# Two weight conversions leave the attention stage, and the joint unit's masks and operands are loaded later

## The chip, the cores and the metric

One core of a Trainium2 chip runs the program. The metric is device time in microseconds of that core. The engines are called PE (TensorE, matmuls), DVE (VectorE), ACT (ScalarE), POOL (GpSimd) and SP (SyncE, which here only issues DMAs).

## What is computed

Causal block attention in blocks of 64 positions (4 batches, 8 heads, 576 positions, 64 per head), then two feed-forward stages on the 2304 x 512 result:

```
scores = scale * q @ k^T, masked where block_i < block_j; attn = softmax(scores)
x  = (attn @ v), heads side by side                          # 4 x 576 x 512
k  = max((mu_k*x + (1-mu_k)*x_prev) @ w_k, 0)                # 512 -> 1024
r  = sigmoid((mu_r*x + (1-mu_r)*x_prev) @ w_r)
x  = r * (k*k @ w_v)                                         # 1024 -> 512
out = x + max(layernorm(x)*g @ w_ch1, 0) @ w_ch2             # 512 -> 2048 -> 512
```

Inputs and output are float32. Most matmuls are done as three passes over a high part and a low part of each operand (high x high, high x low, low x high), so every weight and every activation has to be split into two tiles before PE can use it.

## The kernel before, in words

**Attention** runs as 34 units in a hand-written order (the loop over i from line 973 on). A unit is one head of one batch, except unit 0 and unit 15, which are "z" units: they hold the first 64 positions of all heads of a batch. Unit 15 is the **joint unit**, with batches 1, 2 and 3 in one. In turn i the kernel emits the score product of unit i+1 (em_A), the low-part correction of unit i with its exponential (em_B, ACT tile e), the row maxima of unit i+1 (chain: DVE tiles part, r, m, then the product on DVE line 451 that writes the maxima into QK or, for the joint unit, into wv), the product with V (em_PV), and the split of the operands of the units i+2 and i+3 on POOL (line 44, tiles QK and kq). The heads' operands arrive by DMAs on POOL's queue (line 257, tile kq, two heads at a time) and on SP's queue (tiles raw and V).

The joint unit borrows the tiles of the weight w_v, which are free until after attention: KZ lies in wv[0] and its low parts LZ and QZ in wv[1]. Its **masks** (masks_z, line 236; the DMA is line 237) are one POOL DMA into the lower 64 partitions of LZ and QZ. Each of its three **operands** a = 1, 2, 3 (joint_z, line 294) takes a POOL DMA (line 301), two SP DMAs (lines 302 and 303), an ACT copy and two subtractions, one on POOL and one on DVE or POOL. MASKS_Z and READY_Z (lines 910 and 911) name the turns at which these are emitted: load, ACT copy, the first subtraction, the second subtraction, and the engines of the two.

**Weight conversion.** A weight matrix is cut into pieces of 128 x 512. load_split (line 86) makes of one piece the steps load (an SP DMA of 512 KB into a byte buffer raw), above and below (two reads of the exponent byte), expo, bits (DVE line 135), high and low. During attention above, below and high run on ACT, expo and low on POOL, and bits on DVE. Behind attention above runs on DVE (line 117), below on ACT into PSUM, expo and bits on DVE (lines 129 and 135), high and low on POOL (lines 139 and 44). PIECES (line 904) says at which turns of attention the steps of the first eight pieces are emitted: one letter a turn, l load, 1 and 2 above and below, x expo, b bits, h high, w low (V is low on DVE). The pieces come in the order w_r (four), w_k columns 0 to 511 (four, rows k = 0 to 3), w_k columns 512 to 1023 (four), w_v (eight).

The pieces that PIECES does not name are converted behind attention by a small pipeline (Convert, line 152): each conv.step() advances every piece under way by one step, oldest first, and starts the next. A piece started at step n has its low part emitted at step n+4. These steps stand between the products: six of w_r (em_r), four of w_k for the first group of tokens (em_h, two column blocks m0 to m0+1 each, with out_h behind it: three ACT passes and the DVE subtraction of line 44, tile k), and the first product with w_v (em_v0), which calls step(m) ahead of each of its eight row blocks m. xq.step() in the same places advances prep, which forms the next group's inputs (tiles mix and y). Then the second feed-forward stage runs to the end.

```
def step(self, start=True, keep=0):
    for j in self.going:
        if len(j) > keep:
            f = j.pop(0)
```

Of the kernel before, what the change touches and what calls it, by code (L numbers as in the profile page):

```python
# [32 lines left out]
def attention_moe_kernel(ctx, tc, raw_d, dup_d, raw0_d, dup0_d, v_d, v0_d, msk_d, mz_d, vec_d, eye_d, wk_d, wv_d, wr_d, wc1_d, wc2_d, out_d):  # L33
    nc = tc.nc
# [169 lines left out]
    V = [cp.tile([128, 5, 256], F32, name=f"V{i}") for i in range(2)]  # L204
# [25 lines left out]
    T = {}  # L230

    def masks(i):
        nc.gpsimd.dma_start(out=QK[i][64:128], in_=msk_d)
        nc.gpsimd.memset(KL[i].bitcast(F32)[0:64, 576:640], 0.0)
# [324 lines left out]
    def preps(g, c, X):  # L559
        return [lambda kk=kk: prep(g, kk, c, X) for kk in range(4)]  # L560
# [323 lines left out]
    def em_c2(c, G, ts):  # L884
# [17 lines left out]


    PIECES = [
        (1, "l.12xbhw"), (4, "l12xbhw"), (7, "l..12xbh.w"), (17, "l12xbhw"),
        (20, "l.12xbhw"), (23, "l12xb.hw"), (25, "L.12xb.hw"), (29, "l12xbhV"),
    ]


    MASKS_Z = 2  # L910
    READY_Z = (5, 8.5, 9.5, 9.25, nc.gpsimd, nc.vector), (8, 12, 11.5, 11.25, nc.gpsimd, nc.vector), (10, 13, 14, 13, nc.gpsimd, nc.gpsimd)
    TAIL_Z = 18, 18, 18.5, 20, 23, 22.5, 21, 23.9, 22.9, 21.9
    with tc.manual_schedule():

        plan = {}
        T["attention"] = True
        for i, p in PIECES:
            load, (above, below), (expo, bits), high, low = jobs.pop(0)
            steps = {"l": load, "1": above, "2": below, "x": expo, "b": bits, "h": high, "w": low, "L": load, "V": lambda low=low: low(nc.vector)}
            for x, c in enumerate(p):  # L920
                if c != ".":
                    plan.setdefault(i + x + {"b": .25, "L": .5, "V": .5}.get(c, 0), []).append(steps[c])
        conv = Convert(jobs)
        load_raw(units[0])
        load_raw(units[1])
# [43 lines left out]
        masks(0)  # L969
        plan.setdefault(MASKS_Z, []).append(lambda: masks_z(1, 2))  # L970
        for a in (1, 2, 3):
            joint_z(a, READY_Z[a - 1])
        for i in range(N + 2):
# [23 lines left out]
            if i == N - 2:  # L997
# [8 lines left out]
                xq = Convert(rest)  # L1006
# [52 lines left out]
            if late:  # L1059
                take_z(units[i - 2], 2)  # L1060
                L = tail_z(units[i - 2])
                for a in sorted(set(TAIL_Z)):
                    plan[a] = [f for x, f in zip(TAIL_Z, L) if x == a] + plan.get(a, [])
            if 1 <= i < N - 1 and not mid:
                em_PV(units[i - 1])
                if i == 1:
                    take_z(units[0], 0)
                    L = tail_z(units[0])
# [39 lines left out]
        xq = Convert(preps(2, MR, XC) + preps(3, MR, XD) + preps(4, MR, XA) + preps(5, MR, XC) + preps(HORD[0], MK, XB))  # L1108
        for g, X in enumerate((XA, XB, XC, XD, XA, XC)):
            s = em_r(X)  # L1110
            if g > 1:
                out_r(g - 1, s0)
            xq.some(2)
            if g == 0:
                out_r(g, s)
            if g == 5:

                es_xa.close()
                rh = opened(es_xa, "rh", 3)
                a, b = lambda: rh.tile([128, 4096], I8, name="rawh"), lambda: stg2.tile([128, 4096], I8, name="raw8")  # L1120
                T["raws"] = [a, a, a, b, b, a]
                conv.ahead()
            if g:
                conv.step()
            xq.some(2)
            if g in (2, 4, 5):
                conv.step()
            s0 = s
        xq.all()
# [2 lines left out]
        for j, g in enumerate(HORD):  # L1132
            for m0 in (0, 2, 4, 6):
                s = em_h(X2[j % 2], m0)
                if j == 0 and m0 == 0:
                    out_r(NG - 1, s0)
                out_h(m0, s)
                if j == 0:
                    conv.step()
                    if m0 == 0:  # L1140
                        conv.step()
                if j + 1 == NG and m0 == 0:
                    ln_scale(0, 3 * g)
                    ln_scale(3 * g + 3, NTILE)
            if j + 1 == NG:
                break
            xq = Convert(preps(HORD[j + 1], MK, X2[(j + 1) % 2]))
            if j == 0:

                def step(m):  # L1150
                    if m < 3:
                        conv.step()
                    if m == 1:
                        es_xa.close()
                        xa = opened(es_x, "xa2")
                        X2[1].extend(xa.tile([128, 4, GT], F32R, name=f"y{j}") for j in range(2))
                    xq.step()

                p = em_v0(step)
                assert not conv.jobs and not conv.going and not T["raws"]  # L1160
                T["beside"] = False
                xq.all()
                for t in range(3):
                    out_v(g, t, p[t])
                load_r(HORD[3], rp)
                continue
            em_v(g, 0)
            xq.all()
            if j + 2 == NG:
                conv = Convert(chunk_jobs(0))  # L1170
                conv.some(2, keep=2)
            em_v(g, 1)
            if j + 2 == NG:
                conv.some(2, start=False, keep=2)
            em_v(g, 2)
            if j < 2:
                load_r(HORD[j + 3], rp)
            elif j + 2 == NG:
                load_r(HORD[j + 1], rp)
# [7 lines left out]
        g = HORD[-1]  # L1187
# [257 lines left out]
```

## Time and profile before

| | |
|---|---|
| median of 3 runs | 833.28 us (833.15 to 833.73) |
| the profiled execution's own time | 833.41 us |
| its span, first to last instruction | 831.3 us |
| PE busy | 797.0 us (96%), 3774 matmuls |
| DVE, ACT, POOL busy | 562.9, 410.7, 342.0 us |
| granted TensorE clock | 1.00 over the whole span |

The span falls into attention (to about 181 us), the products with w_r (to 231), w_k for the first group (to 249), the first product with w_v (to 265) and the rest, in which PE is nearly without a gap. In the timelines a row is an engine's instruction or a merged run of like ones; the bracket behind it tells how long the engine stood idle before it and what ended that. In the chain of waits each row is the piece of work on which the end hung in that stretch.

### The profile page before, as it was taken

What the parts mean: (1) busy time and instruction counts of PE and PEld (TensorE: products, weight loads), DVE (VectorE), ACT (ScalarE), POOL (GpSimd) and SP (SyncE); (2) the same over time, 40 slices, a digit from 0 to 9 for tenths busy, and PEclk for the clock granted to TensorE, in tenths of its full rate; (3) what the DMA queues carried; (4) which work ended last, traced back from release to release, by engine and by line L of the source; (5) the groups of instructions that cost most, each with busy time, mean ns of one, the idle gap of its engine ahead of it and who ended that gap; (6) DMA issues with size and microseconds to landing.
All of it is one profiled execution on the core that took longest, in us unless ns stands there. A gap on an engine that the chain in (4) does not pass through costs nothing.

```text
span 831.3 us, 10607 instructions
## 1 busy us (share of the span) xinstructions
PE 797.0 (96%) x3774; PEld 660.9 (80%) x3774; DVE 562.9 (68%) x1011; ACT 410.7 (49%) x700; POOL 342.0 (41%) x303
## 2 busy tenths in 40 slices
PE   3988899999999999999999999999999999999998
PEld 3666666668898998998988887888888888878886
DVE  6889799987788334244386768768575677757545
ACT  6887788878774534525544423233241334343211
POOL 5797889956585011011021659432080630010100
PEclk9999999999999999999999999999999999999999
DMA  8998788821340110012424111604024166160443
GB/s 216 308 335 272 220 259 253 271 83 76 113 178 28 62 64 25 13 39 69 160 95 170 51 52 52 252 24 162 18 102 151 51 205 250 52 236 18 149 155 127
DMA packets 47636, 112.60 MB, mean 135 GB/s; under 512 B 5408, under 2 KB 19872, under 8 KB 45280
## 3 DMA queue, kind: packets, MB, share of 16 engines
q1 hardware_dynamic: 37792, 64.40, 23.8%
q0 software_dynamic: 9360, 45.17, 16.0%
q10 hardware_dynamic: 432, 2.36, 0.7%
q8 instruction: 30, 0.49, 0.2%
q14 instruction: 22, 0.18, 0.1%
HBM read 91.62 MB, written 20.30 MB: 135 GB/s over the span
## 4 chain that ended last, share of the span: by engine, by line
PE 71%; DVE 14%; ACT 8%; issue 4%; DMA 1%; POOL 1%; ACTq 0%; SPq 0%; DVEq 0%; POOLq 0%
PE ph L363 22%; PE po L363 21%; PE s L363 16%; PE p L363 11%; DVE part L418 5%; ACT r L41 2%; ACT e L41 2%; DVE mix L553 1%; DVE QK L451 1%; DVE a L135 1%; DMA raw<-in_raw_dram 1%; PE ph L714 1%; ACT p L41 1%; DVE m L449 1%; DVE acc L896 1%
## 5 line engine op out<-in xcount | busy, mean ns | idle before, releaser
L363 PE MATMUL po<-c,h 128*128 128x512 f32 x864 | 207.9, 392 | 1.7 <-DVE acc L896 1.1
L363 PEld LDWEIGHTS po<-c,h 128*128 128x128 f32 x864 | 161.0, 188 | 39.6 <-DVE acc L896 5.3
L363 PE MATMUL ph<-x,c 128*128 128x512 f32 (+1 forms) x552 | 116.6, 353 | 0.0
L896 DVE TENSOR_TENSOR acc<-po,acc 128x512 f32<-128x512 f32 x144 | 94.7, 685 | 23.0 <-PE po L363 21.9
L363 PEld LDWEIGHTS ph<-x,c 128*128 128x128 f32 x552 | 91.4, 188 | 15.3
L363 PE MATMUL p<-e,V 128*128 128x512 f32 (+1 forms) x310 | 89.4, 435 | 0.0
L363 PE MATMUL p<-wv,k 128*128 128x512 f32 x360 | 82.9, 390 | 0.0
L363 PEld LDWEIGHTS p<-e,V 128*128 128x128 f32 x310 | 54.6, 190 | 30.8 <-issue 25.9
L363 PEld LDWEIGHTS p<-wv,k 128*128 128x128 f32 x360 | 67.4, 188 | 13.8
L44 DVE TENSOR_TENSOR k<-a,k 128x768 fp32r<-128x768 f32 x24 | 23.8, 991 | 73.4 <-ACT a L41 73.4
L41 ACT ACTIVATE h<-ph 128x512 fp32r<-128x512 f32 (+1 forms) x53 | 28.2, 532 | 89.1 <-PE ph L363 89.1
L41 ACT ACTIVATE a<-raw,ce 128x512 f32<-128x512 int8 (+1 forms) x80 | 57.7, 753 | 18.5 <-DVE a L135 10.9
L418 DVE TRANSPOSE_TENSOR_REDUCE part<-s 128x14 f32<-128x448 f32 (+4 forms) x160 | 65.1, 468 | 1.6 <-PE s L363 0.7
L41 ACT ACTIVATE u<-ph 128x512 f32<-128x512 f32 x27 | 16.1, 596 | 87.6 <-PE ph L363 86.3
L41 ACT ACTIVATE e<-s 128x1536 f32<-128x1536 f32 (+1 forms) x34 | 48.4, 1423 | 11.3 <-PE s L363 6.1
L363 PE MATMUL s<-x,wk 128*128 128x384 f32 x288 | 51.7, 338 | 0.9 <-POOL x L44 0.7
L363 PEld LDWEIGHTS s<-x,wk 128*128 128x128 f32 x288 | 50.7, 188 | 1.8 <-POOL x L44 1.0
L363 PE MATMUL s<-y,wk 128*128 128x384 f32 x288 | 51.2, 338 | 0.0
L363 PEld LDWEIGHTS s<-y,wk 128*128 128x128 f32 x288 | 50.8, 188 | 0.2
L814 POOL DMA_DIRECT2D s<-s_scr x12 | 6.4, 535 | 108.0 <-PE ph L363 108.0
L41 ACT ACTIVATE a<-s 128x768 f32<-128x768 f32 x24 | 19.5, 813 | 63.2 <-PE s L363 60.8
L44 POOL TENSOR_TENSOR x<-mix,x 128x384 fp32r<-128x384 f32 x18 | 18.9, 1058 | 75.1 <-ACT x L41 71.3
(178 smaller groups left out, 1410.8 us busy)
## 6 DMA issues: line engine op xcount, KB each, us to landing
kq<-in_dup_dram POOLq DMA_DIRECT2D x15, 1088.0 KB, 7.0
s<-s_scr POOLq DMA_DIRECT2D x13, 1024.0 KB, 7.0
raw<-in_raw_dram SPq DMA_DIRECT2D x32, 288.0 KB, 5.3
raw<-in_w_ch_dram SPq DMA_DIRECT2D x16, 511.6 KB, 3.5
raw<-in_w_ch_dram SPq DMA_DIRECT2D x32, 255.6 KB, 3.9
V<-in_v_dram SPq DMA_DIRECT2D x16, 320.0 KB, 6.4
s_scr<-s POOLq DMA_DIRECT2D x5, 1024.0 KB, 6.3
x_scr<-r SPq DMA_DIRECT2D x18, 256.0 KB, 2.0
```

Of the source, the lines that this page charges most:

```text
L41: nc.scalar.activation(out=out, in_=in_, func=func, **kw)
L44: eng.tensor_tensor(out=out, in0=in0, in1=in1.bitcast(F32), op=ALU.subtract)
L135: stt(out=st["a2"].bitcast(I32), in0=w3, scalar=5, in1=st["a1"].bitcast(I32), op0=ALU.logical_shift_right, op1=ALU.bitwise_or)
L363: nc.tensor.matmul(out=out, lhsT=lhsT, rhs=rhs, start=start, stop=stop, **kw)
L418: red(out=pt[0:kp, b0:b0 + w // 32, j], in_=v3(s[0:kp, o:o + w]), axis=AX.X, op=ALU.max, apply_transpose=True)
L449: lambda: red(out=m, in_=r4[0:32, :, 0:ng], axis=AX.X, op=ALU.max),
L451: lambda x=x: tt(out=v3(dst)[:, x:x + 16], in0=m[:, x:x + 16].unsqueeze(2).to_broadcast([32, 16, 32]), in1=s[64:96, 512:544].unsqueeze(1). ...
L553: stt(out=m[:, o:o + w], in0=XT[b][:, kk, q0:q0 + w], scalar=omm[:, c + kk:c + kk + 1], in1=y[:, o:o + w], op0=ALU.mult, op1=ALU.add)
L714: nc.tensor.transpose(out=pt[kk][:, 128 * x:128 * x + 128], in_=z[:, 128 * kk:128 * kk + 128], identity=eye)
L814: nc.gpsimd.dma_start(out=SF[i].bitcast(F32), in_=s_scr[PAIRS.index(pr), i])
L896: tt(out=acc[i], in0=p, in1=acc[i], op=ALU.add)
```

## The change

MASKS_Z goes from 2 to 12. Of the joint unit's operands, a = 1 has its three loads one turn later and its ACT copy at 10 instead of 8.5; a = 2 has its loads and both subtractions one turn later; a = 3 stays. PIECES loses its entries at 7 and at 29, so the pieces behind the second move up one place each (the entry at 17 now takes the third piece of w_r, and so on) and the pieces k = 2 and 3 of w_k's first columns are left to the pipeline behind attention, which has 14 pieces instead of 12. Of the pipeline's steps eight stood beside the products with w_r, five behind the blocks of w_k and three in the first product with w_v; now it is seven, five and six, and in that last product prep starts one row block later.

```diff
     PIECES = [
-        (1, "l.12xbhw"), (4, "l12xbhw"), (7, "l..12xbh.w"), (17, "l12xbhw"),
-        (20, "l.12xbhw"), (23, "l12xb.hw"), (25, "L.12xb.hw"), (29, "l12xbhV"),
+        (1, "l.12xbhw"), (4, "l12xbhw"), (17, "l12xbhw"),
+        (20, "l.12xbhw"), (23, "l12xb.hw"), (25, "L.12xb.hw"),
     ]
-    MASKS_Z = 2
-    READY_Z = (5, 8.5, 9.5, 9.25, nc.gpsimd, nc.vector), (8, 12, 11.5, 11.25, nc.gpsimd, nc.vector), (10, 13, 14, 13, nc.gpsimd, nc.gpsimd)
+    MASKS_Z = 12
+    READY_Z = (6, 10, 9.5, 9.25, nc.gpsimd, nc.vector), (9, 12, 12.5, 12.25, nc.gpsimd, nc.vector), (10, 13, 14, 13, nc.gpsimd, nc.gpsimd)
...
-                T["raws"] = [a, a, a, b, b, a]
+                T["raws"] = [a, a, a, b, b, a, a, b]
                 conv.ahead()
             if g:
                 conv.step()
             xq.some(2)
-            if g in (2, 4, 5):
+            if g in (2, 4):
                 conv.step()
...
                 def step(m):
-                    if m < 3:
+                    if m < 6:
                         conv.step()
-                    if m == 1:
+                    if m == 3:
                         es_xa.close()
...
-                    xq.step()
+                    if m:
+                        xq.step()
```

PE's order does not change. Two places of the other engines' order follow; a number behind a tile's name tells tiles of one name apart.

POOL, turns 10 to 13 of attention, before (kq and QK are the heads' splits, XT<-XT,RB scales a finished head, wv_84 and wv_83 are the joint unit's tiles, a_698 is a piece's expo):

```order
L44 TENSOR_TENSOR kq<-raw,kq 64x512
L511 TENSOR_TENSOR XT_92<-XT_92,RB_128 128x512
L511 TENSOR_TENSOR XT_92<-XT_92,RB_129 128x512
L44 TENSOR_TENSOR wv_84<-XT_95,wv_83 64x512
L44 TENSOR_TENSOR QK_137<-raw,kq 64x576
L44 TENSOR_TENSOR kq<-raw,kq 64x512
L257 DMA kq<-in_dup_dram 128x2x1088
L131 TENSOR_TENSOR a_698<-a_698,a_743 128x512
L44 TENSOR_TENSOR QK_138<-raw,kq 64x576
L44 TENSOR_TENSOR wv_83<-XT_95,wv_83 64x512
```

The same place in the change:

```order
L44 TENSOR_TENSOR kq<-raw,kq 64x512
L511 TENSOR_TENSOR XT_92<-XT_92,RB_128 128x512
L511 TENSOR_TENSOR XT_92<-XT_92,RB_129 128x512
L44 TENSOR_TENSOR QK_137<-raw,kq 64x576
L44 TENSOR_TENSOR kq<-raw,kq 64x512
L257 DMA kq<-in_dup_dram 128x2x1088
L237 DMA wv_84<-in_mz_dram 64x2x1024
L44 TENSOR_TENSOR wv_84<-XT_95,wv_83 64x512
L44 TENSOR_TENSOR QK_138<-raw,kq 64x576
L44 TENSOR_TENSOR wv_83<-XT_95,wv_83 64x512
```

The subtraction of operand 2 is behind the pair's DMA instead of three instructions ahead of it, the masks' DMA stands right behind that of the pair, and the expo of the piece that started at 7 is gone.

DVE, from the subtraction of the last out_h of the first group on, before (L129 is expo, L135 bits, L117 the next piece's above; mix belongs to prep):

```order
L44 TENSOR_TENSOR k_1868<-a,k_1867 128x768
L129 SCALAR_TENSOR_TENSOR a_2445<-a_2445,p 128x512
L135 SCALAR_TENSOR_TENSOR a_2447<-raw_2368,a_2445 128x512
L117 TENSOR_SCALAR a_2484<-rawh 128x512
L129 SCALAR_TENSOR_TENSOR a_2484<-a_2484,p 128x512
L135 SCALAR_TENSOR_TENSOR a_2486<-rawh,a_2484 128x512
L553 SCALAR_TENSOR_TENSOR mix<-XT_94,omm,mix 128x192
```

The same place in the change, from the third of the pieces that follow that subtraction on (the two ahead of it have the same three rows each):

```order
L129 SCALAR_TENSOR_TENSOR a_2467<-a_2467,p 128x512
L135 SCALAR_TENSOR_TENSOR a_2469<-rawh,a_2467 128x512
L117 TENSOR_SCALAR a_2487<-rawh 128x512
L129 SCALAR_TENSOR_TENSOR a_2487<-a_2487,p 128x512
L135 SCALAR_TENSOR_TENSOR a_2489<-rawh,a_2487 128x512
L117 TENSOR_SCALAR a_2508<-raw_2472 128x512
L553 SCALAR_TENSOR_TENSOR mix<-XT_94,omm,mix 128x192
L553 SCALAR_TENSOR_TENSOR mix<-XT_95,omm,mix 128x192
L129 SCALAR_TENSOR_TENSOR a_2508<-a_2508,p 128x512
L135 SCALAR_TENSOR_TENSOR a_2510<-raw_2472,a_2508 128x512
L553 SCALAR_TENSOR_TENSOR mix<-XT_94,omm,mix 128x192
```

Two pieces stood behind that subtraction before, and five do now, with two of prep's additions between the fourth and the fifth.

## Rows read from the trace of the kernel before

**Rows 1.** Busy us of PE, PEld, DVE, ACT, POOL (count), clock, DMA share, GB/s.
```profile
12.00:84.00 72.00, 62.09 (x284) 45.75 (x285) 62.17 (x156) 57.16 (x106) 58.00 (x53) 1.00 0.96 292
...
231.00:249.00 18.00, 17.10 (x96) 16.46 (x95) 14.73 (x16) 12.12 (x16) 15.75 (x14) 1.00 0.48 179
249.00:265.00 16.00, 16.00 (x72) 13.23 (x71) 13.49 (x19) 8.74 (x18) 11.71 (x11) 1.00 0.01 1
```

**Rows 2.** Chain of waits, turns 11 to 15: start us, us, engine, tile, line.
```profile
71.13 1.58 DVE wv L44
...
76.97 0.96 PE s L363 x5
77.94 2.72 PE p L363 x10
80.66 2.16 PE s L363 x18
...
82.90 1.45 ACT e L41
...
85.43 1.89 DVE wv L451 x3
```

**Rows 3.** ACT timeline, turn 5: start, us, what, [idle before <-releaser].
```profile
40.95 0.76 ACT L41 ACTIVATE a<-raw,ce 128x512 int32<-128x512 int8 x1 [0.89 <-DMA raw<-in_w_r_dram]
```

**Rows 4.** POOL timeline, turn 2.
```profile
22.98 0.64 POOL L237 DMA_DIRECT2D wv<-in_mz_dram  x1
...
29.39 1.27 POOL L44 TENSOR_TENSOR kq<-raw,kq 64x512 fp32r<-64x512 f32 x1 [4.31 <-DMA kq<-in_dup_dram]
```

**Rows 5.** POOL timeline, turn 8.
```profile
53.07 0.58 POOL L301 DMA_DIRECT2D wv<-in_dup_dram  x1
```

**Rows 6.** DVE timeline, turns 8 and 13.
```profile
55.61 1.39 DVE L135 SCALAR_TENSOR_TENSOR a<-raw,a 128x512 int32<-128x512 int32 x1
...
81.21 0.69 DVE L135 SCALAR_TENSOR_TENSOR a<-raw,a 128x512 int32<-128x512 int32 x1
```

**Rows 7.** POOL timeline, turns 11 to 13.
```profile
69.69 1.08 POOL L44 TENSOR_TENSOR wv<-XT,wv 64x512 fp32r<-64x512 f32 x1
...
73.78 0.76 POOL L257 DMA_DIRECT2D kq<-in_dup_dram  x1
...
83.11 1.27 POOL L44 TENSOR_TENSOR kq<-raw,kq 64x512 fp32r<-64x512 f32 x1 [4.71 <-DMA kq<-in_dup_dram]
```

**Rows 8.** DMA issues, 12 to 100 us: count, KB each, median us to landing.
```profile
wv<-in_mz_dram POOLq DMA_DIRECT2D x1, 512.0 KB, 9.1
```

**Rows 9.** PE timeline, the first wv product.
```profile
248.93 16.52 PE L363 MATMUL s<-wv,k 128*128 128x512 f32 x72
```

**Rows 10.** DVE timeline, the wk product and the first wv product.
```profile
238.66 1.34 DVE L44 TENSOR_TENSOR k<-a,k 128x768 fp32r<-128x768 f32 x1 [1.92 <-ACT a L41]
...
254.37 1.02 DVE L135 SCALAR_TENSOR_TENSOR a<-raw,a 128x512 int32<-128x512 int32 x1
255.42 0.43 DVE L117 TENSOR_SCALAR a<-rawh 128x512 f32<-128x512 int8 x1
255.95 0.69 DVE L129 SCALAR_TENSOR_TENSOR a<-a,p 128x512 int32<-128x512 f32 x1
256.74 1.52 DVE L135 SCALAR_TENSOR_TENSOR a<-rawh,a 128x512 int32<-128x512 int32 x1
258.18 2.82 DVE L553 SCALAR_TENSOR_TENSOR mix<-XT,omm,mix 128x192 f32<-128x192 f32 x4
```

**Rows 11.** Tile wv, 228 to 266 us: duration ns min/median/max, first and last start.
```profile
L139 POOL TENSOR_SCALAR wv<-a x8: 626/851/854, 236.4 to 258.3; 128x512 fp32r<-128x512 f32 x8
L44 POOL TENSOR_TENSOR wv<-a,wv x8: 1300/1598/2094, 237.3 to 259.2; 128x512 fp32r<-128x512 f32 x8
```

**Rows 12.** POOL timeline, the first wv product.
```profile
256.41 1.31 POOL L44 TENSOR_TENSOR wv<-a,wv 128x512 fp32r<-128x512 f32 x1
...
259.15 1.30 POOL L44 TENSOR_TENSOR wv<-a,wv 128x512 fp32r<-128x512 f32 x1
```

More of the change, by code (lines that the diff above doesn't have):

```diff
@@ L918, in attention_moe_kernel @@
             load, (above, below), (expo, bits), high, low = jobs.pop(0)
-            steps = {"l": load, "1": above, "2": below, "x": expo, "b": bits, "h": high, "w": low, "L": load, "V": lambda low=low: low(nc.vector)}
+            steps = {"l": load, "1": above, "2": below, "x": expo, "b": bits, "h": high, "w": low, "L": load}
             for x, c in enumerate(p):
                 if c != ".":
-                    plan.setdefault(i + x + {"b": .25, "L": .5, "V": .5}.get(c, 0), []).append(steps[c])
+                    plan.setdefault(i + x + {"b": .25, "L": .5}.get(c, 0), []).append(steps[c])
         conv = Convert(jobs)
```

## The prediction

> **What bounds the kernel now.** I read the busy times by stage first, to see where PE has gaps at all. In attention it has: from 12 to 84 us PE is busy 62.09 of 72 us, DVE 62.17 and POOL 58.00, with the DMA engines at 0.96 [rows 1]. Under the first w_k product it has 17.10 of 18 us, and under the first w_v product 16.00 of 16 [rows 1]. So an earlier finish in attention is a gain, and behind attention only a new wait can change the time.
>
> Next the chain of waits, to see what fills attention. It runs over DVE and ACT in a ring: row maxima, copies, maxima again, the product with the maxima, then the next unit. A DVE instruction put between two units lengthens the ring whole: operand 2's subtraction stands in the chain with 1.58 us [rows 2]. Where the joint unit's scores come in, the chain runs over PE instead: 0.96, 2.72 and 2.16 us from the correction of unit 13 to that of unit 14, then ACT's exponential at 82.90, and at 85.43 DVE writes the joint unit's maxima into wv [rows 2].
>
> Last the timelines of DVE and POOL under the first w_v product. What the reader is to see there is that the two hold each other up: bits takes 0.69 us with POOL idle [rows 6], and 1.52 beside POOL, where it ends 0.54 us after POOL's low part [rows 10, 12].
>
> **What the change does in attention.**
>
> *Early loads.* The masks' DMA leaves turn 2. There POOL stood 4.31 us for a pair of heads that competed with it [rows 4], and three turns later ACT stood 0.89 us for a weight piece, just ahead of an exponential on the chain [rows 3]. With 512 KB [rows 8] less to move, the whole queue runs ahead. The 0.89 is the most it can give, 0 the least, if the piece is late for its own reasons; I take 0.4. POOL's issue of the masks, 0.64 us [rows 4], was hidden in its idle time.
>
> *Turn 8.* Operand 2's DMA issue (0.58 us of POOL [rows 5]) leaves the place ahead of the split that held bits up: 1.39 us there against 0.69 with POOL idle [rows 6]. The gain is 0 to 0.7; I take 0.4. ACT's moved copy and the SP loads of the first and second operands have turns to spare: nothing.
>
> *Turns 11 to 13.* Operand 2's DVE subtraction leaves turn 11, which frees 1.58 us, and returns in turn 12. There the ring of unit 14 gets it, while PE's own chain of 0.96, 2.72 and 2.16 us [rows 2] has become the longer one. If it costs nothing beyond PE's chain, the exponential of unit 14 comes 1.6 earlier. If it takes 1.58 again, unit 14's maxima start where they do now; the piece's bits (0.69 at 81.21 [rows 6]) lies behind them and isn't waited for, and PE's correction then ends 0.6 us earlier, since it no longer queues behind 2.72 and 2.16. I take 1.0. POOL loses operand 2's subtraction of 1.08 in turn 11 and an expo, gains the masks' issue and that subtraction in turn 12, and then stands 4.71 us for a pair anyway [rows 7]: no cost.
>
> *The piece at 29.* Its bits and its low part lie behind the last correction, from which on PE has no gap until the w_k product; its ACT steps at turns 30 and 31 stand ahead of exponentials that wait for PE. Nothing. The same goes for the high and low parts of the piece at 7, in turns 14 and 16. Together attention gives 1.8 us, with bounds of 0.6 and 3.2.
>
> **What it does behind attention.** w_k's two extra pieces come first and are in time: their low parts are emitted beside the products with w_r. But every later piece is late by them. Behind the last out_h subtraction of the first group stood two pieces, and now five, as the order shows. POOL ended the last low part of w_v at 259.15 + 1.30 = 260.45 [rows 12]. PE takes 16.52 / 8 = 2.07 us for each row block of w_v [rows 9], so it needs that last part at 248.93 + 7 x 2.07 + 0.2 = 263.6: a margin of 3.2 us. In the change the piece that ends at that place is k = 4, and three follow.
>
> Each costs a period of DVE and POOL together: from the end of bits at 254.37 + 1.02 to that at 256.74 + 1.52, 2.87 us [rows 10]. POOL makes high, then low, and the next bits ends only 0.54 us after low. The last period also holds two of prep's additions; four of them took 2.82 us [rows 10], so two are 1.4, of which I take 0.9, as part lies beside POOL's copies. On the other side POOL is idle when out_h's first subtraction comes, because its next high part has to wait for a bits behind it: the 1.34 us subtraction and the 1.02 us bits beside it [rows 10] each lose an estimated 0.3 (bits' 1.02 against 0.69 [rows 6]). So the last low part lands at 260.45 - 0.6 + 2 x 2.87 + 3.77 = 269.4 in this trace's time, and PE waits 269.4 - 263.6 = **5.8 us** in all, spread over the row blocks k = 2 to 7.
>
> Bounds: the least is a piece at DVE's own pace, 0.43 + 0.69 + 0.69 [rows 6, 10] and some 0.3 between, 2.1 us. Three of these with the additions free leave 260.45 - 0.6 + 6.3 - 263.6 = 2.6. The most is 2.87 a piece with 1.4 and without the 0.6: 6.9. I stay at 5.8, since two periods in a row show 2.87 in the very place that is now repeated. Prep's late inputs for the next group are covered by the same wait, and the second stage has room.
>
> By the Trainium skill (SBUF — State Buffer, "Who interferes with whom") the later of two such instructions on VectorE and GpSimd blocks until the earlier has finished. By that rule the four instructions of a piece would stand in a row, and the sum would come out 0.9 us higher, as worked out at the second rival. The trace doesn't bear out the full block: beside POOL bits ends 0.54 us after the low part, sooner than the 0.69 it needs alone [rows 6, 10, 12].
>
> **Sum.** 833.41 - 1.8 + 5.8 = 837.4 for the profiled execution, which lies 0.13 above the median; so **837.3 us**. The bounds are 833.41 - 3.2 + 2.6 = 832.8 and 833.41 - 0.6 + 6.9 = 839.7.
>
> **The rivals.**
>
> *The masks land late.* They are now issued behind a pair's DMA at 73.78 + 0.76 [rows 7], or 1.1 us sooner for the missing subtraction. Their DMA took 9.1 us from issue to landing [rows 8], so they land at 82.6 to 83.6. DVE needs them at 85.43 [rows 2] less the gain of 1.8, at 83.6. The pair ahead of them was waited for until 83.11 [rows 7]. If they land 1.8 us late, ahead of everything else on DVE, attention gives nothing: 839.1 us. It decides from a landing after 83.6. The Trainium skill (DMA: Bandwidth & Descriptors, "Issuing engines are not separate DMA queues") says that all DMAs interleave on the same engines; that makes the pair and the masks slow each other, as the 9.1 us also show.
>
> *A full block.* If above, high, low and bits of a piece each wait for the one before, a piece costs 0.43 [rows 10] + 0.63 + 1.30 [rows 11] + 0.69 [rows 6] + 0.1 between = 3.15 us instead of 2.87. Three pieces add 0.9: 838.2. The 0.54 us speaks against it. This is what the Trainium skill's rule on the two engines (SBUF — State Buffer, "Who interferes with whom") would do here.
>
> *DVE gets its turn: no change or better.* The mechanism is the same hold between DVE and POOL. If the shifted order lets bits go ahead of POOL's low part, a piece costs 2.1 us instead of 2.87, and the subtraction in turn 12 and bits in turn 8 cost little: 832.8 - 0.1 = 832.7. It decides if the period falls under some 2.3 us and attention gives over 2.5. For it: bits did take 0.69 [rows 6]. Against it: that was with POOL idle, and POOL has eight pairs of copies to make, at 1.30 us at the least for low alone [rows 11].
>
> *The late pieces aren't late:* PE isn't made to wait for w_v, because some other queue holds it where it is. Then only attention counts: 833.28 - 1.8 = 831.5. Against it stands PE's full 16.00 of 16 us [rows 1].
>
> **How the numbers follow.** My forecast has 0.57, the late masks 0.15, the full block 0.10, DVE's turn 0.13, no lateness 0.05. The range goes from 834.3 to 839.7: it leaves out the last two and takes in the first three with their terms' bounds, the low end for a gain near 3 with a wait near 4. A change of 0.2% is 1.7 us, about what a measurement can tell. Faster by more: 0.05, most of the last case. Within: 0.11, most of DVE's turn. Slower: 0.84.
>
> **What would show it.** PE between its first w_k product and the end of the first w_v product should last some 6 us longer, with waits for POOL's wv parts, and DVE's bits there at 2.9 us from one to the next. The last correction of attention should come 1 to 2 us earlier, with the 0.89 us wait on ACT gone or smaller. I am wrong if PE stays without a gap under w_v, or if attention's end moves by more than 3.2 us or later. A wait of DVE for the masks would speak for the first rival.

## The result, and the profile after

| | before | after |
|---|---|---|
| median of the runs | 833.50 us (4 runs) | 840.01 us (838.79 to 842.26, 4 runs) |
| profiled execution's own time, span | 833.41, 831.3 us | 840.63, 838.7 us |
| mean granted TensorE clock | 1.00 | 0.995 |

The ratio is 1.0073, with a 95% interval of 1.0047 to 1.0099. The change is slower, as forecast, but by 6.5 us (by 6.1 if one goes by the ratio) instead of 4.0. The median lies 0.3 us above the upper end of the range; the ratio, times the 833.28 us from which the forecast started, gives 839.4, just inside it.

To see where the 7.4 us of span come from I follow three marks through both traces: ACT's last exponential of attention, and the starts of the first w_k and the first w_v product on PE. First the timeline of ACT, its exponentials (tile e) of units 14, 15, 16 and 33. Before:

```profile
82.90 1.45 ACT L41 ACTIVATE e<-s 128x1536 f32<-128x1536 f32 x1 [1.41 <-PE s L363]
...
89.50 1.45 ACT L41 ACTIVATE e<-s 128x1536 f32<-128x1536 f32 x1
...
93.75 1.45 ACT L41 ACTIVATE e<-s 128x1536 f32<-128x1536 f32 x1 [0.80 <-DVE rs L506]
...
176.37 1.45 ACT L41 ACTIVATE e<-s 128x1536 f32<-128x1536 f32 x1 [0.98 <-DVE mix L553]
```

The same four after the change:

```profile
80.30 1.45 ACT L41 ACTIVATE e<-s 128x1536 f32<-128x1536 f32 x1 [0.80 <-PE s L363]
...
90.39 1.45 ACT L41 ACTIVATE e<-s 128x1536 f32<-128x1536 f32 x1 [0.94 <-PE s L363]
...
96.24 1.45 ACT L41 ACTIVATE e<-s 128x1536 f32<-128x1536 f32 x1 [0.98 <-PE s L363]
...
178.82 1.45 ACT L41 ACTIVATE e<-s 128x1536 f32<-128x1536 f32 x1 [0.99 <-DVE mix L553]
```

Unit 14 comes 2.60 us earlier, unit 15 0.89 later, unit 16 2.49 later, and the last one 2.45 later. The promised gain was there up to unit 14, and was more than lost at the joint unit, unit 15. At unit 0, ahead of all that the change moves in attention, this trace stands 0.46 us earlier already, and those of the other runs stand between 0.58 earlier and 0.11 later; so a shift between two traces is good to about half a microsecond.

Then PE's timeline from the w_k product on. Before (the w_v product between the last two rows is in [rows 9]):

```profile
230.60 3.51 PE L363 MATMUL s<-x,wk 128*128 128x384 f32 x19
234.83 1.14 PE L363 MATMUL s<-x,wk 128*128 128x384 f32 x5 [0.72 <-POOL x L44]
236.15 12.94 PE L363 MATMUL s<-x,wk 128*128 128x384 f32 x72 [0.18 <-ACT r L41]
...
265.29 10.02 PE L363 MATMUL s<-y,wk 128*128 128x384 f32 x56
```

After the change (left out are five more rows of the w_v product, each behind a wait for POOL's wv):

```profile
233.05 17.05 PE L363 MATMUL s<-x,wk 128*128 128x384 f32 x96
249.94 4.51 PE L363 MATMUL s<-wv,k 128*128 128x512 f32 x19
255.62 2.33 PE L363 MATMUL s<-wv,k 128*128 128x512 f32 x9 [1.17 <-POOL wv L44]
...
270.89 2.10 PE L363 MATMUL s<-wv,k 128*128 128x512 f32 x8 [0.88 <-POOL wv L44]
272.83 2.45 PE L363 MATMUL s<-y,wk 128*128 128x384 f32 x13
```

The w_k product lost its two small waits: 249.94 - 233.05 = 16.89 us instead of 248.93 - 230.60 = 18.33, a gain of 1.44. The w_v product takes 272.83 - 249.94 = 22.89 us instead of 16.36, a loss of 6.53, and every wait in it is for POOL's wv parts. The waits in the brackets add up to 4.50 us; the other 2.0 lie in the rows themselves, 18.54 us for the 72 matmuls that took 16.52, since a run that starts behind a wait is longer than its share (2.33 us for 9 matmuls, 2.07 before). 2.45 - 1.44 + 6.53 = 7.54 us, and 0.1 is given back in the rest of the program.

**The joint unit.** The chain of waits of the changed kernel now runs through the masks' DMA (start us, us, what):

```profile
71.25 14.74 DMA wv<-in_mz_dram
...
86.02 1.30 DVE wv L451 x2
...
87.36 2.93 PE s L363 x13
```

On DVE's timeline the wait stands in the middle of the rows that write the maxima into wv:

```profile
82.84 0.69 DVE L451 TENSOR_TENSOR wv<-mz,s 32x512 fp32r<-32x512 f32 x1
86.02 1.29 DVE L451 TENSOR_TENSOR wv<-mz,s 32x512 fp32r<-32x512 f32 x2 [2.50 <-DMA wv<-in_mz_dram]
```

The masks were issued at 71.25, more than 2 us sooner than the prediction's first rival had it, and took 14.74 us from issue to landing, not the 9.1 of [rows 8]. The DMA page of 60 to 90 us shows that the pairs and the small broadcasts RB around them took longer too (count, KB each, median us to landing). Before:

```profile
kq<-in_dup_dram POOLq DMA_DIRECT2D x2, 1088.0 KB, 7.3
RB<-n_scr SPq DMA_DIRECT2D x4, 128.0 KB, 4.2
```

After:

```profile
kq<-in_dup_dram POOLq DMA_DIRECT2D x2, 1088.0 KB, 9.7
RB<-n_scr SPq DMA_DIRECT2D x4, 128.0 KB, 10.6
wv<-in_mz_dram POOLq DMA_DIRECT2D x1, 512.0 KB, 14.7
```

And the late masks set off a second loss. PE's timeline at the joint unit's correction, before:

```profile
87.38 1.61 PE L363 MATMUL s<-wv 128*128 128x128 f32 x13 [1.09 <-DVE wv L451]
88.83 2.86 PE L363 MATMUL p<-e,V 128*128 128x512 f32 x10
```

After:

```profile
87.36 2.93 PE L363 MATMUL s<-wv 128*128 128x128 f32 x13 [3.42 <-DVE wv L451]
90.09 4.54 PE L363 MATMUL p<-e,V 128*128 128x512 f32 x10
```

The correction starts when it did before (87.36 against 87.38), so the lateness ate just the gain. But PE had stood idle for 3.42 us, and the same 13 and 10 matmuls then took 2.93 and 4.54 us instead of 1.61 and 2.86. The windows of the changed kernel show the clock (columns as in [rows 1]):

```profile
12.00:84.00 72.00, 65.28 (x295) 48.54 (x295) 61.28 (x156) 56.44 (x106) 58.33 (x54) 1.00 0.97 275
84.00:90.00 6.00, 2.63 (x13) 2.64 (x14) 3.92 (x8) 1.33 (x3) 5.57 (x5) 0.72 1.10 327
90.00:96.00 6.00, 6.00 (x23) 3.88 (x22) 2.99 (x9) 3.36 (x6) 2.79 (x4) 0.71 0.22 67
```

Up to 84 us PE had even got through 65.28 us of work, where it was 62.09 [rows 1]. Then the granted clock is 0.72 and 0.71 in two stretches of 6 us, so for a part of each TensorE ran at its lower level, 1.2 GHz. From the start of the correction to the exponential of unit 16 it was 93.75 - 87.38 = 6.37 us before and is 96.24 - 87.36 = 8.88 now, with PE busy without a gap on the same matmuls: 2.5 us that the clock took, the whole of the net loss.

**The first w_v product.** DVE's and POOL's timelines there answer to [rows 10, 12]. DVE:

```profile
257.47 1.51 DVE L135 SCALAR_TENSOR_TENSOR a<-raw,a 128x512 int32<-128x512 int32 x1
259.01 0.43 DVE L117 TENSOR_SCALAR a<-rawh 128x512 f32<-128x512 int8 x1
259.54 0.69 DVE L129 SCALAR_TENSOR_TENSOR a<-a,p 128x512 int32<-128x512 f32 x1
260.33 1.51 DVE L135 SCALAR_TENSOR_TENSOR a<-rawh,a 128x512 int32<-128x512 int32 x1
...
265.10 2.16 DVE L553 SCALAR_TENSOR_TENSOR mix<-XT,omm,mix 128x192 f32<-128x192 f32 x2
```

POOL:

```profile
257.13 1.30 POOL L44 TENSOR_TENSOR wv<-a,wv 128x512 fp32r<-128x512 f32 x1
259.06 0.85 POOL L139 TENSOR_SCALAR wv<-a 128x512 fp32r<-128x512 f32 x1 [0.63 <-DVE a L135]
260.00 1.30 POOL L44 TENSOR_TENSOR wv<-a,wv 128x512 fp32r<-128x512 f32 x1
```

bits ends at 258.98, then at 261.84: the period is 2.86 us, against 2.87 forecast. Read the loop across the two engines: bits ends, POOL makes high (0.85), then low (1.30), and the next bits ends 0.54 us after that low. high seems to be held up as well: above starts 0.05 us ahead of it and takes its 0.43, and high takes 0.85 where, earlier in this trace with DVE idle, it took 0.61:

```profile
236.54 0.61 POOL L139 TENSOR_SCALAR wk<-a 128x512 fp32r<-128x512 f32 x1
```

### The profile page after: what moved, and what is told of

Read it like the earlier page. It is cut to its first block, busy times and chain, and to the rows that moved or that the text cites. A ratio compares the mean times of both kernels' runs of the same rounds, so it can differ in the third digit from the quotient of the medians.

```text
span 838.7 us, 10607 instructions
## 1 busy us (share of the span) xinstructions
PE 802.5 (96%) x3774; PEld 663.6 (79%) x3774; DVE 562.7 (67%) x1014; ACT 409.0 (49%) x696; POOL 342.2 (41%) x304
## 4 chain that ended last, share of the span: by engine, by line
PE 74%; DVE 12%; ACT 5%; DMA 4%; POOL 2%; issue 2%; DVEq 0%; ACTq 0%; POOLq 0%
PE ph L363 22%; PE po L363 20%; PE s L363 19%; PE p L363 12%; DVE part L418 3%; DMA wv<-in_mz_dram 2%; DMA kq<-in_dup_dram 2%; DVE a L135 2%; ACT r L41 1%; ACT e L41 1%; DVE QK L451 1%; ACT a L41 1%; POOL kq L44 1%; PE ph L714 1%; DVE acc L896 1%
## 5 line engine op out<-in xcount | busy, mean ns | idle before, releaser
L363 PE MATMUL p<-e,V 128*128 128x512 f32 (+1 forms) x310 | 91.1, 441 | 0.0
L41 ACT ACTIVATE a<-raw,ce 128x512 f32<-128x512 int8 (+1 forms) x76 | 54.7, 753 | 17.7 <-DVE a L135 10.9
```

The costliest lines, as they stand in the source:

```text
L41: nc.scalar.activation(out=out, in_=in_, func=func, **kw)
L363: nc.tensor.matmul(out=out, lhsT=lhsT, rhs=rhs, start=start, stop=stop, **kw)
```

## The experiments

Each kernel ran in turns with the kernel before on one chip; the ratios are to that, with their 95% intervals. Where I say how far a unit has moved, it is the start of its exponential against the trace of before.

### The masks

**masks_back**, the change with the masks where they were:

```diff
-    MASKS_Z = 12
+    MASKS_Z = 2
```

> The change with its masks loaded in turn 2 again. Theory A (the masks are late: DVE waits 2.5 us for them, PE stands still, and PE runs at its lower clock just after) expects attention to keep the 2.6 us it had gained by unit 14, less about 1.0 that the early turns owe to the masks' absence: 840.0 - 5.0 + 1.0, so 835 to 837 us, and no wait of DVE for the masks. Rival B (the whole DMA queue is overfull at turns 12 and 13, because the operands' loads were moved there, and the masks only show it) expects DVE or PE to wait there for another transfer: 838.5 us or more.

836.05 us (6 runs) beside 832.14, ratio 1.0052 (1.0038 to 1.0067); the change itself had 1.0073. The time is as theory A had it, and no wait for the masks is left. Units 14 and 15 are both 2.54 us earlier and the last one 2.29: the joint unit costs nothing when its masks are there. The w_v product is unchanged, 22.90 us with the same waits. In this run too the granted clock is 0.72 from 84 to 90 us, after PE stood 1.09 us for DVE's wv as in the kernel before, and the gain falls from 2.54 to 1.27 at unit 16.

```profile
84.00:90.00 6.00, 5.15 (x19) 3.30 (x20) 5.59 (x15) 4.11 (x8) 5.85 (x6) 0.72 0.68 232
```

A trace is one execution: extra_step and act_high below have the same attention as this run, and their last unit comes 1.76 us earlier and 1.41 us later than before. The trace of act_high is the slowest of its twelve executions. It falls 2.5 us behind from unit 7 to unit 9, just behind a bits of 1.68 us that takes 0.63 here, and loses another 1.25 at unit 16, with the clock at 0.74 from 90 to 96 us.

**masks_alone**, the kernel before with the late masks and nothing else:

```diff
-    MASKS_Z = 2
+    MASKS_Z = 12
```

> The kernel before with the masks' DMA moved to turn 12 and nothing else. Theory A: the gain of about 1.0 us in turn 5, then masks that land 12 to 15 us after an issue at about 74, so at 86 to 89 us, against a need at about 84.5: a wait of 2 to 4 us and a lower clock behind it, 835 to 838 us in all. Rival B: no late landing without the moved operands, 832.3 to 833.5 us.

835.16 us (830.87 to 839.00, 12 runs), ratio 1.0030 (1.0013 to 1.0048). The median is in A's range, and the spread stands out: no other kernel here varied by 8 us, though the kernel before did by 6.5 in 29 runs of another session. The profiled execution, 832.57 us, is one of the good ones. In it the masks were issued 3.3 us later than in the change, took 11.0 us and landed at 85.60, and unit 15 lost only 0.8 against unit 14. That the spread comes from the moment of this one landing is likely but not shown: only one execution has a trace.

**masks_ahead**, the change with the masks' DMA just ahead of the pair of heads:

```diff
-    MASKS_Z = 12
+    MASKS_Z = 11.9
```

> The changed kernel with the masks' DMA issued just ahead of the pair of heads instead of just behind it. Theory A (attention's loss of some 5 us is the masks' late landing, and it is late because its DMA shares the engines with a pair issued ahead of it): the masks land by 82 us instead of 86.0, DVE no longer waits for them, PE has no gap of 3 us before the joint unit's corrections, and attention ends 1 to 2.5 us earlier than in the kernel before; behind attention the 5.1 us remain, so about 1.004 of the kernel before (835 to 837 us where that takes 832.1 to 833.5). Theory B (the DMA engines are simply full in these turns, the order of the two issues does not count): the masks land after 84 us as before the shift and the ratio stays at 1.007 or above.

838.86 us beside 832.68, ratio 1.0077 (1.0062 to 1.0093): A had the landing right and the time wrong, B the time right and the landing wrong: the masks did land in time, at 80.18. But now the pair of heads landed at 84.54, after 13.4 us, and POOL's split of it made PE wait. From the timeline of POOL, then of PE:

```profile
84.61 1.26 POOL L44 TENSOR_TENSOR kq<-raw,kq 64x512 fp32r<-64x512 f32 x1 [8.67 <-DMA kq<-in_dup_dram]
```

```profile
85.92 1.65 PE L363 MATMUL s<-kq 128*128 128x512 f32 x5 [2.96 <-POOL kq L44]
```

Whichever of the two DMAs is second lands at 84.5 to 86.0 us (masks_alone, the change, this run), and PE stands for it or for what DVE or POOL makes of it; without the masks beside it the pair landed at 80.3 to 83.3 in the other eleven traces, that of the kernel before among them, and PE did not stand for it. The Trainium skill (DMA: Bandwidth & Descriptors, "Issuing engines are not separate DMA queues") has all DMAs interleave on the same engines; these landings agree, and the order of issue only chooses the victim.

**masks_mid** and **masks_turn10**, the change with the masks in turn 7 and in turn 10:

```diff
-    MASKS_Z = 12
+    MASKS_Z = 7.5
```

> The changed kernel with the masks' DMA in turn 7 instead of turn 12, where the load of the piece that started at 7 is gone. Theory A (the loss in attention is that the transfers of turns 9 to 13, to which the change adds the masks' 512 KB, land too late for unit 15 and unit 16; early turns have room): the masks land before 60 us, the pair of turn 12 lands before 82 us, there is no gap of 3 us on PE at 83 to 87 us, attention ends 1.5 to 3.3 us earlier than in the kernel before, and with the 5.1 us behind attention the ratio is 1.002 to 1.005 (masks_back 1.0052, the change itself 1.007). Theory B (any place but turn 2 takes transfers away that someone waits for): a wait of 1 us or more shows up for an operand, a pair or a weight piece between turns 7 and 10, and the ratio stays at 1.006 or above.

```diff
-    MASKS_Z = 12
+    MASKS_Z = 10
```

> The changed kernel with the masks' DMA in turn 10, two turns earlier, ahead of operand 3's load. Theory A (it counts how much the queue carries ahead of the pair of turn 12): the masks land near 70 us, in time, but operand 3 and what follows land about 2 us later than in masks_mid (512 KB at the 250 to 380 GB/s that these turns show are 1.4 to 2 us), and the pair of turn 12 lands at 82 to 84 us, near the point where the scores of unit 16 need it; the ratio is between masks_mid and the change, 1.003 to 1.007. Theory C (only the meeting of the masks with the pair and the four broadcasts of turn 12 counts): as masks_mid, no later landing of the pair, ratio 1.002 to 1.005.

836.78 and 836.46 us beside 831.93, ratios 1.0062 (1.0046 to 1.0079) and 1.0050 (1.0036 to 1.0064). In the traces the A of masks_mid holds for both: the masks land at 57.10 and 71.81, the pair at 80.75 and 81.56, no 3 us gap is left, and the last unit comes 1.47 and 1.46 us earlier than before, at the low end of A's 1.5 to 3.3. The ratio of masks_mid lies above A's band of 1.002 to 1.005, which its interval just reaches. The landing of the pair at 82 to 84 that A gave turn 10 did not show, as C said there. So by the ratios turns 7 and 10 serve as well as turn 2, and of the turns tried turn 12 alone is too late.

### The operands and the pieces

**operands_alone**, the kernel before with the later operands only:

```diff
-    READY_Z = (5, 8.5, 9.5, 9.25, nc.gpsimd, nc.vector), (8, 12, 11.5, 11.25, nc.gpsimd, nc.vector), (10, 13, 14, 13, nc.gpsimd, nc.gpsimd)
+    READY_Z = (6, 10, 9.5, 9.25, nc.gpsimd, nc.vector), (9, 12, 12.5, 12.25, nc.gpsimd, nc.vector), (10, 13, 14, 13, nc.gpsimd, nc.gpsimd)
```

> The kernel before with the new turns of the joint unit's operands and nothing else. Theory A: operand 2's subtraction leaves turn 11 for turn 12, where PE's chain covers it, 0.5 to 1.6 us less: 831.9 to 833.0 us. Rival B: the later loads crowd turns 12 and 13, 834 to 837 us. If what DVE loses to POOL only moves from one turn to another: 833.5 us.

831.14 us (12 runs) beside 832.14, ratio 0.9990 (0.9979 to 1.0001). Unit 13 comes 3.07 us earlier, the last 1.92: by the trace this is the useful part of the change, though here as well the clock took 1.3 us back at unit 16 (0.81 granted from 84 to 90 us). The ratio is 0.8 us in A's direction, with no change still just inside its interval.

**pieces_alone**, the change with masks and operands as before:

```diff
-    MASKS_Z = 12
-    READY_Z = (6, 10, 9.5, 9.25, nc.gpsimd, nc.vector), (9, 12, 12.5, 12.25, nc.gpsimd, nc.vector), (10, 13, 14, 13, nc.gpsimd, nc.gpsimd)
+    MASKS_Z = 2
+    READY_Z = (5, 8.5, 9.5, 9.25, nc.gpsimd, nc.vector), (8, 12, 11.5, 11.25, nc.gpsimd, nc.vector), (10, 13, 14, 13, nc.gpsimd, nc.gpsimd)
```

> The change with the masks and the operands as before, so that only the two weight pieces are moved behind attention. Theory A: PE waits for w_v as in the change, a w_v product some 6.5 us longer and a w_k product 1.4 us shorter, so 5.1 us behind attention, and attention within 0.7 us of that before: 837.9 to 839.3 us. Rival C (the wait for w_v is longer because attention's end came out of step) expects 835 us or less.

838.02 us, ratio 1.0066 (1.0048 to 1.0084), as A had it. Attention ends 0.33 us later, so two conversions fewer give it nothing; w_k has no gap and w_v takes 270.75 - 247.82 = 22.93 us.

### Behind attention

**extra_step** (edits against masks_back): the fourteen pieces get their eighth step beside the w_r products back, so four stand behind the last out_h subtraction instead of five.

```diff
-            if g in (2, 4):
+            if g in (2, 4, 5):
...
-                    if m < 6:
+                    if m < 5:
...
```

> The changed kernel with the masks in turn 2, its fourteen pieces, and the eighth step beside the products with w_r put back (eight, five and five steps instead of seven, five and six), so that four pieces, not five, stand behind the last out_h subtraction and no addition of prep stands between them. Theory A (the lateness is the number of pieces behind that subtraction times 2.87 us): the last low part comes 2.9 to 3.8 us earlier and the first w_v product takes 19.0 to 20.2 us instead of 22.9; the w_k product has its small gaps of before again (18.3 instead of 17.05 us), so the whole is 1.5 to 2.5 us under masks_back. Theory B (DVE and POOL are full from the w_r products on, so the place of a step counts for nothing and only the total does): still 22.5 us or more in the product.

834.00 us beside 832.68, ratio 1.0016 (1.0006 to 1.0026). The w_v product runs from 245.73 to 265.77, 20.04 us, 2.86 less than in masks_back: one period for one piece. Theory B falls. The gaps in the w_k product, which A expected back, did not return, and by the two ratios (1.0052 - 1.0016, times 833) the gain over masks_back is 3.0 us where A had at most 2.5; the two intervals are too wide to tell these apart.

**one_piece** (against masks_back; the buffers' list follows the number of pieces): the piece at 29 goes back into attention, three stand behind that subtraction.

```diff
-        (20, "l.12xbhw"), (23, "l12xb.hw"), (25, "L.12xb.hw"),
+        (20, "l.12xbhw"), (23, "l12xb.hw"), (25, "L.12xb.hw"), (29, "l12xbhV"),
...
-            if g in (2, 4):
+            if g in (2, 4, 5):
...
-                    if m < 6:
+                    if m < 4:
...
```

> The changed kernel with the masks in turn 2 and one piece given back to attention (the one at 29), so that thirteen are left for behind it and three, not five, have their bits behind the last out_h subtraction of the first group. Theory A (the margin of 3.2 us that the kernel before had is real, and each piece costs 2.87 us): the last low part comes 5.7 us earlier than with fourteen pieces, 0.3 us inside the margin, and the first w_v product takes 16.4 to 17.4 us instead of 22.9; the whole stands at 0.998 to 1.000 of the kernel before. Theory B (the waits come from the total work that DVE and POOL have from the w_r products on, with no margin): half of the 6.5 us stays, the product takes 19 to 20.5 us, the ratio is 1.002 to 1.003.

831.93 us (11 runs) beside 832.68, ratio 0.9990 (0.9975 to 1.0005). PE's timeline:

```profile
233.11 13.78 PE L363 MATMUL s<-x,wk 128*128 128x384 f32 x77 [0.86 <-POOL x L44]
246.73 14.70 PE L363 MATMUL s<-wv,k 128*128 128x512 f32 x64
261.70 2.10 PE L363 MATMUL s<-wv,k 128*128 128x512 f32 x8 [0.28 <-POOL wv L44]
263.64 4.40 PE L363 MATMUL s<-y,wk 128*128 128x384 f32 x24
```

The w_v product takes 16.91 us with one wait of 0.28. The margin of 3.2 us that the prediction read is real: with two, three, four and five pieces behind that subtraction (before, one_piece, extra_step, masks_back) the product takes 16.36, 16.91, 20.04 and 22.90 us. The first extra piece is nearly free, and each one after it costs about a period.

**act_high** (against masks_back): in the w_v product ACT makes the high part.

```diff
         def high():
-            if T.get("beside"):
+            if T.get("beside") and not T.get("v0"):
...
+                T["v0"] = True
                 p = em_v0(step)
```

> The changed kernel with the masks in turn 2 (the run masks_back, 1.0052 of before), and in the first w_v product the high part of each piece is made by ACT instead of POOL. Theory A (PE waits there for pieces that cost a period of 2.87 us because DVE and POOL hold each other up, and POOL's high part of 0.85 us is in that period): the period falls to 2.0 us (2.87 - 0.85), and the 22.9 us from the first to the last w_v product of the first group fall to 18.5 to 20.5, 2.5 to 4.5 us less than masks_back. Theory B (the period is set by POOL's low part and bits alone, the high part lies beside them): still 2.87 us a piece and 22.9 us in all. Theory C (the raw loads or PE itself set the pace): no change either, and the waits name DMA or nothing.

834.20 us beside 832.68, ratio 1.0020 (1.0008 to 1.0031). The product fell to 270.27 - 249.20 = 21.07 us, between A and B: the period is 2.60, not 2.0. DVE's timeline, then ACT's and POOL's:

```profile
256.72 1.24 DVE L135 SCALAR_TENSOR_TENSOR a<-raw,a 128x512 int32<-128x512 int32 x1
...
259.32 1.24 DVE L135 SCALAR_TENSOR_TENSOR a<-rawh,a 128x512 int32<-128x512 int32 x1
```

```profile
257.99 0.63 ACT L41 ACTIVATE wv<-a 128x512 fp32r<-128x512 f32 x1 [1.34 <-DVE a L135]
```

```profile
258.70 1.31 POOL L44 TENSOR_TENSOR wv<-a,wv 128x512 fp32r<-128x512 f32 x1 [1.29 <-ACT wv L41]
```

bits ends at 257.96, high runs to 258.62, low to 260.01, and bits ends again at 260.56. The high part stays in the loop, on whatever engine; ACT's is only 0.2 us shorter. A was right that DVE and POOL hold each other, and wrong that one can take high out of the loop by moving it.

**other_piece** (against one_piece): the piece at 7 is the one that goes back.

```diff
-        (1, "l.12xbhw"), (4, "l12xbhw"), (17, "l12xbhw"),
-        (20, "l.12xbhw"), (23, "l12xb.hw"), (25, "L.12xb.hw"), (29, "l12xbhV"),
+        (1, "l.12xbhw"), (4, "l12xbhw"), (7, "l..12xbh.w"), (17, "l12xbhw"),
+        (20, "l.12xbhw"), (23, "l12xb.hw"), (25, "L.12xb.hw"),
```

> As one_piece (thirteen pieces behind attention, later operands, masks in turn 2), but the piece that is given back to attention is the one at 7, not the one at 29. Theory A (the w_k product's waits of 0.86 us for POOL's x in one_piece, and of 0.72 and 0.18 us in the kernel before, come from the piece at 29, whose bits of 1.41 us and low part on DVE stand among prep's additions at the end of attention): the w_k product runs 17.05 us without a gap, the w_v product takes 16.4 to 17.4 us as in one_piece, attention ends within 1 us of one_piece, and the whole is 0.5 to 1.5 us faster than one_piece, ratio 0.997 to 0.9985. Theory B (the gap comes from the order of the steps beside the w_r products, or from thirteen pieces instead of fourteen): the gap of 0.7 to 0.9 us stays, and the ratio is 0.999 to 1.0005.

831.29 us (12 runs) beside 833.35, ratio 0.9977 (0.9963 to 0.9990): faster than the kernel before, and the lowest ratio of all, though its interval overlaps those of one_piece and operands_alone. PE's timeline:

```profile
229.90 17.05 PE L363 MATMUL s<-x,wk 128*128 128x384 f32 x96
246.79 14.80 PE L363 MATMUL s<-wv,k 128*128 128x512 f32 x64
```

The w_k product is without a gap and the w_v product takes 17.14 us, as A expected; attention ends 1.16 us later than in one_piece, a little more than A allowed. The gap stands in the five traces that have the piece at 29 in attention (before, masks_alone, operands_alone, one_piece, one_piece_mid) and in none of the nine without it, so it comes from that piece. How, DVE's timeline of the kernel before shows: that piece's bits and low part stand among prep's additions,

```profile
179.75 1.41 DVE L135 SCALAR_TENSOR_TENSOR a<-raw,a 128x512 int32<-128x512 int32 x1
...
193.92 0.93 DVE L44 TENSOR_TENSOR wk<-a,wk 128x512 fp32r<-128x512 f32 x1
```

and both are absent here. The addition behind the second stands 18.51 us behind the last exponential there and 16.22 here, so they hold up prep by as much as 2.3 us, and the last of prep's inputs is what the w_k product waited for on POOL. In the kernel before, then in the change, which leaves that piece out too:

```profile
233.77 1.01 POOL L44 TENSOR_TENSOR x<-mix,x 128x384 fp32r<-128x384 f32 x1
```

```profile
234.30 1.01 POOL L44 TENSOR_TENSOR x<-mix,x 128x384 fp32r<-128x384 f32 x1
```

It ends 4.18 us behind the start of the w_k product before, 2.26 in the change and 2.38 in this run.

**one_piece_mid** (against one_piece):

```diff
-    MASKS_Z = 2
+    MASKS_Z = 7.5
```

> The kernel of one_piece (thirteen pieces behind attention, later operands) with the masks' DMA in turn 7 instead of turn 2: the parts of the change that gave something, without those that cost. Theory A (turn 2 without the masks is worth 1.0 us at unit 6, and it is kept to the end of attention): 0.5 to 1.5 us faster than one_piece, ratio 0.997 to 0.9985 of the kernel before. Theory B (what is gained early is lost again at the joint unit, where PE's chain sets the time): as one_piece, ratio 0.999 to 1.000.

832.46 us beside 831.93, ratio 1.0006 (0.9991 to 1.0021); nearer to B than to A. The gain that A wanted to keep was hardly there: unit 6 gains 0.36 us against unit 5, and 0.31 in one_piece, and ACT still stands 0.54 us for the weight piece. The last unit comes 1.91 us earlier than before, in one_piece 1.86.

## Why the prediction was right, and where it was not

*Slower, by late pieces of w_v: right.* The term of 5.8 us measured 6.53. The period of 2.87, the margin of 3.2 and the place of the waits all came out. The last low part ended at 269.54 + 1.29 = 270.83, in the frame of before 1.01 less, 269.8, against 269.4 forecast. Two small terms make that difference. The 0.6 us to be saved at out_h's first subtraction came, 0.96 and 0.69 us for it and its bits instead of 1.34 and 1.02, but as the w_k product lost its waits that subtraction stands 0.47 us nearer to the w_v product, and only 0.3 was left at the last one; and the last period took 3.93 us, not 3.77. The rest is that PE needed 2.0 us from there to the end of the product and not 1.7.

*The early loads, 0.4 us (bounds 0 and 0.89): under-sized where it arose.* ACT's wait of 0.89 is gone, and unit 6 gained 1.0 against unit 5. But masks_turn10, with the same 1.0 at unit 6, ends attention only 1.46 us earlier, where masks_back and extra_step, with their masks in turn 2, have 2.29 and 1.76. Nothing of it is seen at the end.

*Turn 8, 0.4 us: as forecast.* bits took 0.88 us there instead of 1.39, a gain of 0.5.

*Turns 11 to 13, 1.0 us: right in kind, 1.6 in size.* Operand 2's subtraction on DVE took 0.70 us in turn 12, not 1.58, and unit 13 gained 1.6 against unit 12.

*"Together attention gives 1.8 us": wrong, and this is the step that failed.* It rests on the "no cost" at POOL's part of turn 12, which left the masks' landing to a rival with a chance of 0.15. They landed at 86.00, behind the 83.6 from which that rival decides. Its working used the 9.1 us of [rows 8], from a turn with less beside it; in turn 12 the pair, the broadcasts and the masks were in flight together and all took longer, and it was 14.74. Why it was 3.7 us more than in masks_alone, which has the same meeting, stays open. The rival's price, the loss of the whole gain, was right as far as it went (2.6 us up to unit 14, none at the correction). What the prediction did not price is that PE then ran on at a lower clock, which cost 2.5 us more. In place of a gain of 1.8 us attention lost 2.45. With masks in time attention gives 1.5 to 2.3 us in the traces of masks_mid, masks_turn10, masks_back and extra_step, which is the 1.8 of the forecast, but act_high's trace shows that an execution can miss it; by operands_alone (1.92) and pieces_alone (none) it comes from the operands.

*The piece at 29, "nothing": wrong.* I looked only at PE behind the last correction, though [rows 1] show 0.90 us without a matmul in the w_k product's stretch. Its bits and low part delayed prep, and without it the w_k product was 1.44 us shorter. That the total came out near the forecast is in part luck: this gain, which was put at nothing, hides a part of attention's miss of 4.25 us.

*Full block.* The period stayed at 2.86, so the rival's 3.15 is out. Its mechanism is nearly right. bits needs 0.69 us alone and ended 0.54 behind low, so all but 0.15 of it waited; above takes its 0.43, and high, which starts 0.05 behind it, takes 0.85 instead of 0.61. From the start of above to the end of high it is 0.90 us, where one behind the other would be 1.04. Some 0.15 us of overlap at each of these two places is the difference between 3.15 and 2.86. The Trainium skill's rule (SBUF — State Buffer, "Who interferes with whom"), by which the one that comes later is blocked until the earlier has finished, agrees with the trace but for these 0.15 us.

*DVE's turn, and no lateness:* both out, by the 2.86 and by PE's waits.

## What to carry to other kernels

Before a load is moved later, add up what else is in flight there and take its landing time from that stretch, not from where it stands now; a landing read in a quieter stretch says little of the moment when several meet. Where one engine hands tiles to another and is held up by it in turn, the two run at the length of their loop: count the pieces that are added behind the last free moment, multiply by the loop, and subtract the margin. A step that is off the critical path can still stand ahead of one that feeds a later stage, so follow its engine to the next product before costing it at nothing.

## What the runs showed of the hardware that was not expected

The masks' DMA of 512 KB took 9.1 to 10.6 us from issue to landing in turns 2, 7 and 10, 9.7 just ahead of the pair of turn 12, and 11.0 and 14.7 behind it. That pair, 1088 KB, took 7.2 to 10.4 us without the masks beside it and 10.6 to 13.4 with them.

After a wait of 3.42 us PE's granted clock fell to 0.72 (in masks_ahead, after 2.96, to 0.64) and the next matmuls took up to 1.8 times as long (2.93 against 1.61 us), so that a late tile was paid for twice. But in masks_back, masks_mid and operands_alone the clock fell too (0.72 to 0.81 from 84 to 90 us, 1.3 us lost), after waits of 1.09 to 1.30 us, while in extra_step, one_piece and masks_turn10 it stayed at 1.00 after the same 1.09 us, in other_piece after 1.30 and in masks_alone after 1.45. The Trainium skill (TensorE: Matmul & The Clock Gate, "What's actually happening") says that the rate follows how busy PE has been recently; the two long waits agree with that much. What told the outcomes of the short ones apart stays open.
